# Moving a 192-byte tile ahead of four pools, so that the tiles behind it begin 192 bytes later

## The chip, the cores and the metric

The kernel runs on one core of one Trainium2 chip. The metric is the device time of one execution in microseconds (us). Before the change the median of three runs is 416.2 us (415.88 to 416.37).

## The reference

The kernel computes a gated mix of an attention branch and a dense branch over 2048 tokens of 448 features, all in float32:

```python
g = sigmoid((x * gate_w).sum(-1, keepdims=True))
# branch A: 16 heads of 28; each token attends to the 8 tokens 0, 2, 4 ... 14 places back
qkv = x @ wqkv;  logits = q . k[pos - 2*w] * 28**-0.5;  a = (softmax(logits) . v) @ wo
# branch B
h = relu(x @ w1 + b1) ** 2;  b = h @ w2 + b2          # 448 -> 1792 -> 448
out = g * a + (1 - g) * b
```

## The kernel before, in words

Precision and pairs. Every matrix product is made of three: each operand is split into a high part (`...h`) and a low part (`...l`, or index 1 of a token tile), and high x high, high x low and low x high are added up in PSUM. The contraction of 448 is cut into seven pieces of 64 rows. `side_by_side` (lines 308 to 317) issues two matmuls at a time, one on rows 0 to 63 of TensorE and one on rows 64 to 127, which run beside each other. Below, such a couple is a **pair step**. Line 315 is `nc.tensor.matmul(acc.pt[:, :acc.n], a[rows], w[rows], ...)`: `a` is the stationary operand, which a weight load (LDWEIGHTS) brings into the array, and `w` is the moving operand, which is streamed past it, 448, 450 or 512 columns long.

The stages on TensorE, in order:

- q, k and v (`qkv_first`, `qkv_two`, `run`): four chunks of 512 tokens, of 252 matmuls each (chunk 0: 36 over all 128 rows at line 402, then 180). Stationary: 128 tokens of a chunk's tiles `x{c}_{j}`. Moving: `wqh`, `wql`, `w7h`, `w7l`, 448 columns, or 450 for q, where two columns carry the gate's weights. Chunk 3 has the first steps of the dense branch ahead of its last 24 matmuls.
- The dense branch, in the chunk order 3, 0, 1, 2 (`ORDER`). `h_first` and `h_second`: stationary `w1h`, `w1l`, `w17h`, `w17l`, moving the chunk's token tiles, 512 columns: 4 x 147 = 588 pair steps. `o_part`: stationary the tiles `h{c}_{f}`, moving `w2ah`, `w2al`, `w2bh`, `w2bl`, 448 columns.
- The attention's output times `wo` (`wo_first`, `wo_second`, `wo_end`): stationary the split heads, moving `woh`, `wol`, `wo7h`, `wo7l`, 448 columns.

Beside TensorE, GpSimd (POOL) multiplies q with k (`qk_piece`, line 504) and the weights with v (`av_piece`, line 516) into tiles `pp`, VectorE (DVE) reduces them (lines 508 and 526), ScalarE (ACT) evacuates PSUM and splits operands. Transfers are issued by the SP queue. A planner (`Plan`) with a table of costs writes the order of the instructions out while the program is built; sizes and dependences go into it, addresses don't.

Where tiles lie. Pools are laid out one behind the other in SBUF, in the order of their opening, and a tile's address is the same in all partitions. `const` begins at byte 1152, which is 128 modulo 256, and is 77,312 bytes long, a multiple of 256. Behind it lie `xpool`, `attp`, `smp`, `prodp`, `smallp` (only `zg`, 6 x 8 floats, 192 bytes) and `rawp`. Lines 277 (`pad_a`), 952 (`pad_b`) and 443 (48 floats in `kv_tile`) are fillings of 192 bytes. In the program as built the starts are, modulo 256:

| tiles | role on TensorE | start before | start after |
|---|---|---|---|
| `w1h`, `w1l`, `w17h`, `w17l` | stationary, dense branch | 128 | 128 |
| `w2ah`, `w2al`, `w2bh`, `w2bl`, `woh` ... `wo7l` | moving | 128 | 128 |
| `wqh`, `wql`, `w7h`, `w7l`, all three blocks | moving, q, k, v | 128 | 128 |
| `x0_j`, `x2_j` (pool `phase_a_x`) | stationary, q, k, v | 64 | 64 |
| `x1_j`, `x3_j` (pool `xpool`) | stationary, q, k, v; `x3_j` also moving | **128** | **64** |
| `x0b_j`, `x1b_j`, `x2b_j` in `xpool` | moving, dense branch | **128** | **64** |
| `x0b_3`, `x1b_0`, `x2b_2` (pool `weights_b`) | moving, dense branch | 128 | 128 |
| `h{c}_{f}` (pool `rawp`), `oh`, `ol`, `o7` | stationary | 64 | 64 |
| `o...` in the `pp` tiles, lines 1043 and 1044 | stationary | 64 | 64 |
| q, k, v tiles, `lg`, `pp` | none | **128** | **64** |

Slices of 128 tokens, of 128 columns of `w1`, and the blocks of `wqh` begin at multiples of 256 bytes, so they keep these remainders. The reloaded tokens `x{c}b_j` take the four slots of `xpool` and a fifth one in `weights_b` in turn (`x_reload`, line 945).

Of the kernel before, what the change touches and what calls it, by code (L numbers as in the profile page):

```python
# [7 lines left out]
F32 = mybir.dt.float32  # L8
F32R = mybir.dt.float32r
# [4 lines left out]
S, D, H, DH, W, F = 2048, 448, 16, 28, 8, 1792  # L14
P = 128
NS = 8
# [4 lines left out]
C = HG * DH  # L21
# [16 lines left out]
PP_BUFS = 4  # L38
# [15 lines left out]
class Plan:  # L54
# [29 lines left out]
    def add(self, eng, cost, fn, *deps, prio=MID, at=0.0, port=False, move=None):  # L84
        j = Job()
        j.eng, j.cost, j.fn, j.deps, j.prio, j.port, j.move = eng, cost, fn, [d for d in deps if d], prio, port, move
        j.at, j.done, self.count = max(at, self.now), None, self.count + 1
        j.n = self.count
        self.jobs[eng].append(j)
        return j  # L90
# [88 lines left out]
def gated_mix_kernel(ctx: ExitStack, tc: tile.TileContext, xT, wqkv, w1, w2, wo, b1, b2, out):  # L179
    nc = tc.nc  # L180

    def f32(ap):
        return ap.bitcast(F32)
# [12 lines left out]
    const = ctx.enter_context(tc.tile_pool(name="const", bufs=1))  # L196
# [8 lines left out]
    w2al = const.tile([P, NFA, D], F32R, name="w2al")  # L205
    b2t = const.tile([P, D], F32, name="b2t")
    mask = const.tile([P, NS, W], F32, name="mask")

    xpool = ctx.enter_context(tc.tile_pool(name="xpool", bufs=1))
    attp = ctx.enter_context(tc.tile_pool(name="attp", bufs=1))  # L210
    smp = ctx.enter_context(tc.tile_pool(name="smp", bufs=2))
    prodp = ctx.enter_context(tc.tile_pool(name="prodp", bufs=1))
    smallp = ctx.enter_context(tc.tile_pool(name="smallp", bufs=1))
    zg = smallp.tile([P, 6, NS], F32, name="zg")
    zt, gt, g1t = zg[:, 0:2], zg[:, 2:4], zg[:, 4:6]
    rawp = ctx.enter_context(tc.tile_pool(name="rawp", bufs=2, reuse_waits="tile"))
    biasp = ctx.enter_context(tc.tile_pool(name="biasp", bufs=1))
# [761 lines left out]
    def fin_fetch(par, t):  # L979
        if (par, t) in half:  # L980
            fin_begin(par, t)
# [51 lines left out]
    def wo_split(par, t, hold, loads):  # L1033
        st = Wo()
        st.par, st.t = par, t
        place = "pp" if par and t % 4 else "oh"
        st.place = place
        free = part_last["oh"] if place == "oh" else reduced_all[-PP_BUFS:] + part_last["pp"]
        st.accs = accs = [Acc("m", f"a{par}_{t + r}", D, now=False) for r in range(2)]

        def parts():
            if place == "pp":
                oh, ol, o78 = (prodp.tile([P, C * W], F32R, tag="pp", name=f"o{n}{par}_{t}", bufs=PP_BUFS)[:, 48:48 + n * P]
                               for n in (6, 6, 2))
            else:
                oh, ol, o78 = (bp.tile([P, n * P], F32R, tag=tag, name=f"{tag}{par}_{t}")
                               for tag, n in (("oh", 6), ("ol", 6), ("o7", 2)))
            st.oh, st.ol = (o.rearrange("p (k t n) -> p k t n", k=3, t=2) for o in (oh, ol))
            st.o7, st.o8 = o78[:, :P], o78[:, P:]
            raw = hold[0]  # L1050
            st.full, st.last = raw[:, :6 * P].rearrange("p (k t n) -> p k t n", k=3, t=2), raw[:, 6 * P:]
            nc.scalar.activation(st.oh, st.full, AF.Copy)

        def copied(r):
            accs[r].open()
            st.pv = getattr(st, "pv", []) + [accs[r].pt.rearrange("p (k n) -> p k n", k=4)]
            nc.scalar.activation(st.pv[r][:, 0:3], st.full[:, :, r], AF.Copy)

        a = add(ACT, 847.0, parts, *loads, *free, prio=SOON)
        b = [add(ACT, 486.0, lambda r=r: copied(r), a, *accs[r].after, prio=SOON) for r in range(2)]  # L1060
        b[1].deps.append(b[0])
        c7 = add(ACT, 293.0, lambda: nc.scalar.activation(st.o7, st.last, AF.Copy), b[1], prio=SOON)
        d7 = add(ACT, 262.0, lambda: nc.scalar.activation(st.pv[0][:, 3], st.last, AF.Copy), c7, prio=SOON)
        lows = [add(DVE, 550.0, lambda r=r: nc.vector.tensor_sub(st.ol[:, :, r], st.pv[r][:, 0:3], f32(st.oh[:, :, r])),
                    b[r], prio=SOON) for r in range(2)]
        lows.append(add(DVE, 280.0, lambda: nc.vector.tensor_sub(st.o8, st.pv[0][:, 3], f32(st.o7)), d7, prio=SOON))
        if not par or t == 0:
            raw_last["ot"] = [d7]
        for r in range(2):
            fin_fetch(par, t + r)  # L1070
        st.jobs = [d7, *lows]
        accs[0].after, accs[1].after = (*st.jobs,), (*st.jobs,)
        return st
# [119 lines left out]
    for g in range(2, 2 * NF):  # L1193
        i, f = g // (NF // 2), g % (NF // 2) * 2
# [111 lines left out]
```

## Time and profile before

| | |
|---|---|
| median of three runs | 416.2 us (415.88 to 416.37) |
| the profiled execution's own time | 415.95 us |
| its span, first to last instruction | 414.1 us |
| TensorE matmuls busy | 408.6 us, 3828 matmuls |
| VectorE, ScalarE, GpSimd busy | 258.6, 206.0, 265.8 us |
| mean granted TensorE clock | 0.999 |

The page gives the busy time of each engine, then the span in 40 slices, the chain of work that ended last, and the costliest groups of instructions with the mean duration of one. [...]

### The profile page before, as it was taken

Reading aid. Unit: us, or ns where it says so; the run is one execution under the profiler, and the core shown is the slowest. Engines: PE = TensorE matmul, PEld = TensorE weight load, DVE = VectorE, ACT = ScalarE, POOL = GpSimd, SP = SyncE. Lnnn points to the kernel's source line nnn. Section 1 sums busy time; section 2 is a strip of 40 time slices with the busy share of each in tenths; the row PEclk is TensorE's granted clock in tenths of the full one; section 3 lists DMA queues with packets and bytes.
Section 4 is the critical chain, followed back from the end, with each engine's and each line's share of the span. In section 5 each row is a group of like instructions: output and inputs, shape, how many; then the busy total and the mean of one; then the engine's idle time right before and its main releaser. Section 6 shows DMA issues by size and latency. Waiting matters only on the chain.

```text
span 414.1 us, 9249 instructions
## 1 busy us (share of the span) xinstructions
PE 408.6 (99%) x3828; PEld 404.2 (98%) x3828; DVE 258.6 (62%) x346; ACT 206.0 (50%) x501; POOL 265.8 (64%) x165
## 2 busy tenths in 40 slices
PE   8999999999999999999999999999999999999996
PEld 7999999999999999999999999999999999999995
DVE  4514523484386768777656899786767586593453
ACT  5746766242464665444555435345615344346730
POOL 0000000876969999889999897999998975950000
PEclk9999999999999999999999999999999999999999
DMA  7999999845164433544203669663626022068404
GB/s 242 377 346 295 398 378 372 309 156 205 46 215 188 150 106 132 208 161 152 82 4 127 223 149 310 218 162 64 218 91 232 4 90 85 22 158 157 112 2 178
DMA packets 64555, 73.75 MB, mean 178 GB/s; under 512 B 32321, under 2 KB 57345, under 8 KB 64129
## 3 DMA queue, kind: packets, MB, share of 16 engines
q1 hardware_dynamic: 64224, 72.90, 53.5%
q8 instruction: 30, 0.49, 0.5%
q10 hardware_dynamic: 288, 0.26, 0.2%
q14 instruction: 13, 0.10, 0.1%
HBM read 45.71 MB, written 28.25 MB: 179 GB/s over the span
## 4 chain that ended last, share of the span: by engine, by line
PE 98%; DMA 1%; DVE 0%; ACT 0%; issue 0%
PE b L315 32%; PE h L315 32%; PE qkv L315 23%; PE a L315 7%; PE qkv L402 2%; PE a L1096 1%; DMA wqraw<-wqkv 1%; DVE bt_b L987 0%; ACT wqh L796 0%
## 5 line engine op out<-in xcount | busy, mean ns | idle before, releaser
L504 POOL TENSOR_TENSOR pp<-q,k 128x896 f32<-128x896 f32 x64 | 135.1, 2152 | 86.9 <-DMA k<-k_d 78.4
L516 POOL TENSOR_TENSOR pp<-lg,v 128x896 f32<-128x896 f32 x64 | 118.9, 1962 | 4.3 <-DVE lg L508 2.6
L315 PE MATMUL qkv<-wqh,x 64*128 64x448 f32 (+1 forms) x528 | 91.6, 362 | 0.0
L757 DVE TENSOR_TENSOR h<-h,h 128x512 fp32r<-128x512 f32 x56 | 38.7, 691 | 67.2 <-ACT h L756 66.8
L315 PE MATMUL b<-w2ah,h 64*128 64x448 f32 x448 | 78.8, 359 | 0.0
L315 PE MATMUL b<-w2bh,h 64*128 64x448 f32 x448 | 78.7, 359 | 0.0
L508 DVE TENSOR_REDUCE lg<-pp 128x32 f32<-128x896 f32 x64 | 67.5, 1077 | 14.0 <-POOL pp L504 14.0
L315 PE MATMUL qkv<-wql,x 64*128 64x448 f32 (+1 forms) x264 | 75.2, 362 | 0.0
L315 PEld LDWEIGHTS qkv<-wqh,x 64*128 64x128 f32 x528 | 74.0, 184 | 0.3
L526 DVE TENSOR_REDUCE o<-pp 128x112 f32<-128x896 f32 x64 | 67.2, 1069 | 3.1 <-POOL pp L516 3.1
L315 PEld LDWEIGHTS b<-w2ah,h 64*128 64x128 f32 x448 | 63.8, 184 | 0.0
L315 PEld LDWEIGHTS b<-w2bh,h 64*128 64x128 f32 x448 | 62.9, 184 | 0.2
L315 PE MATMUL b<-w2al,h 64*128 64x448 f32 x224 | 63.1, 358 | 0.0
L315 PE MATMUL b<-w2bl,h 64*128 64x448 f32 x224 | 62.3, 358 | 0.0
L753 ACT ACTIVATE h<-h,b1z 128x512 f32<-128x512 f32 x56 | 36.7, 656 | 41.1 <-PE h L315 41.1
L315 PEld LDWEIGHTS qkv<-wql,x 64*128 64x128 f32 x264 | 44.7, 184 | 0.2
L315 PEld LDWEIGHTS b<-w2al,h 64*128 64x128 f32 x224 | 38.4, 184 | 0.0
L315 PEld LDWEIGHTS b<-w2bl,h 64*128 64x128 f32 x224 | 37.7, 184 | 0.1
L315 PE MATMUL h<-x,w1h 64*128 64x512 f32 x168 | 35.7, 386 | 0.0
L315 PE MATMUL h<-x0b,w1h 64*128 64x512 f32 x168 | 35.6, 386 | 0.0
L337 ACT ACTIVATE st<-qkv 128x448 f32<-128x448 f32 x48 | 24.4, 541 | 21.8 <-PE qkv L315 15.8
L755 ACT ACTIVATE h<-h 128x512 fp32r<-128x512 f32 x56 | 33.5, 598 | 1.5
(132 smaller groups left out, 855.6 us busy)
## 6 DMA issues: line engine op xcount, KB each, us to landing
k<-k_d SPq DMA_DIRECT2D x8, 840.0 KB, 6.1
v<-v_d SPq DMA_DIRECT2D x8, 840.0 KB, 4.7
x_d<-x SPq DMA_DIRECT2D x12, 512.0 KB, 6.4
q_d<-st SPq DMA_DIRECT2D x8, 448.0 KB, 4.8
k_d<-st SPq DMA_DIRECT2D x8, 448.0 KB, 4.7
v_d<-st SPq DMA_DIRECT2D x8, 448.0 KB, 5.5
q<-q_d SPq DMA_DIRECT2D x8, 448.0 KB, 3.3
o_d<-o SPq DMA_DIRECT2D x16, 224.0 KB, 2.2
```

The source lines that it names most:

```text
L315: nc.tensor.matmul(acc.pt[:, :acc.n], a[rows], w[rows], start=acc.todo == acc.all, stop=acc.todo == 1)
L337: nc.scalar.activation(st[0][:, :, t % 2], pt[:, :D].rearrange("p (g c) -> p g c", g=G), AF.Copy)
L402: nc.tensor.matmul(acc.pt[:, :NQ], a, w, start=k == j == 0, stop=False)
L504: nc.gpsimd.tensor_mul(pr.rearrange("p (w c) -> p w c", w=W), q[:, s:s + 1].to_broadcast([P, W, C]), k[:, s:s + W])
L508: nc.vector.tensor_reduce(lgs[i][:, s], pr.rearrange("p (w h d) -> p w h d", w=W, h=HG), axis=AX.X, op=ALU.add)
L516: nc.gpsimd.tensor_mul(pr.rearrange("p (h d w) -> p w h d", h=HG, w=W), lgs[i][:, s][:, :, :, None].to_broadcast([P, W, HG, DH]), vs[i][:, ...
L526: nc.vector.tensor_reduce(o_t[par, s][:, g * C:(g + 1) * C], pr.rearrange("p (c w) -> p c w", w=W), axis=AX.X, op=ALU.add)
L753: a = add(ACT, 656.0, lambda pt=pt, r=r: nc.scalar.activation(pt, pt, AF.Relu, bias=b1t[:, f + r:f + r + 1]), ready, bias_job[0], prio=NEXT)
L755: b = add(ACT, 600.0, lambda pt=pt, hh=hh: nc.scalar.activation(hh, pt, AF.Square), a, prio=NEXT)
L757: low = add(DVE, 690.0, lambda pt=pt, hh=hh, hl=hl: nc.vector.tensor_sub(hl, pt, f32(hh)), a, prio=NEXT)
L1096: nc.tensor.matmul(acc.pt[:, :D], a, w, start=False, stop=acc.todo == 1)
```

## The change

`zg` is allocated at the end of `const` and no longer in a pool of its own behind `prodp`. So `xpool`, `attp`, `smp` and `prodp` begin 192 bytes later, and `rawp` and all behind it stay where they were. The heads that `wo_split` keeps in `pp` tiles lose their offset of 48 floats, so that their addresses stay as they were too. The order of the instructions on each engine, their sizes and their waits are the same before and after: the two programs differ in addresses alone.

```diff
     mask = const.tile([P, NS, W], F32, name="mask")
+    zg = const.tile([P, 6, NS], F32, name="zg")
 
     xpool = ctx.enter_context(tc.tile_pool(name="xpool", bufs=1))
     attp = ctx.enter_context(tc.tile_pool(name="attp", bufs=1))
     smp = ctx.enter_context(tc.tile_pool(name="smp", bufs=2))
     prodp = ctx.enter_context(tc.tile_pool(name="prodp", bufs=1))
-    smallp = ctx.enter_context(tc.tile_pool(name="smallp", bufs=1))
-    zg = smallp.tile([P, 6, NS], F32, name="zg")
     zt, gt, g1t = zg[:, 0:2], zg[:, 2:4], zg[:, 4:6]
...
             if place == "pp":
-                oh, ol, o78 = (prodp.tile([P, C * W], F32R, tag="pp", name=f"o{n}{par}_{t}", bufs=PP_BUFS)[:, 48:48 + n * P]
+                oh, ol, o78 = (prodp.tile([P, C * W], F32R, tag="pp", name=f"o{n}{par}_{t}", bufs=PP_BUFS)[:, :n * P]
                                for n in (6, 6, 2))
```

## The prediction

> **What bounds the kernel now.** The page first: span, busy time, granted clock, and the chain that ended last.
>
> ```profile
> span 414.1 us, 9249 instructions
> ...
> PE 408.6 (99%) x3828; PEld 404.2 (98%) x3828; DVE 258.6 (62%) x346; ACT 206.0 (50%) x501; POOL 265.8 (64%) x165
> ...
> PEclk9999999999999999999999999999999999999999
> ...
> PE 98%; DMA 1%; DVE 0%; ACT 0%; issue 0%
> ```
>
> TensorE has 98% of the chain at an ungated clock. The view of TensorE's waits shows whether something else makes it late:
>
> ```profile
> PE warm L771 <- DVE b1z L768: 1.1, 1, 1.1
> PE qkv L402 <- ACT wqh L796: 0.3, 1, 0.3
> ```
>
> Two waits, 1.4 us, both before the first pair step. From there the end is set by the pace of the pair steps alone, and a change that moves nothing but addresses can act in two ways: by that pace, or by slowing another engine until TensorE must wait for it. The profiled execution took 415.95 us, 1.85 more than its span; the three runs have a median of 416.2.
>
> The chain in order of time gives the pace where nothing disturbs it (dense branch, chunk 1):
>
> ```profile
> 270.33 2.40 PE b L315 x24
> ...
> 274.54 2.72 PE h L315 x24
> 277.26 2.40 PE b L315 x24
> ```
>
> 24 matmuls are 12 pair steps: 200 ns with 448 columns and 226.7 ns with 512. The 64 more columns cost 26.7 ns, 0.417 ns each; 448 x 0.417 is 186.7 and 512 x 0.417 is 213.3, so either form pays the same 13.3 ns beside its columns. Now the four chunks of q, k and v, by windows (stretch, its length, then TensorE's busy time and matmuls, which count those cut by the edges). The first lies inside chunk 0; the second and third run from the first matmul of chunks 1 and 2 to that of the next, found by counting 252; the fourth from the first of chunk 3 to the first of the dense branch, 228 on:
>
> ```profile
> 18.00:30.00 12.00, 12.00 (x123) 12.00 (x122) 2.60 (x5) 6.19 (x18) 0.00 (x0) 1.00 0.95 341
> 31.04:56.78 25.74, 25.74 (x256) 25.63 (x253) 10.33 (x19) 16.66 (x52) 0.00 (x0) 1.00 1.01 355
> 56.78:82.15 25.37, 25.37 (x254) 24.93 (x253) 10.03 (x15) 13.91 (x44) 8.50 (x5) 1.00 0.97 347
> 82.15:105.54 23.39, 23.39 (x231) 23.39 (x228) 15.68 (x10) 8.47 (x29) 17.24 (x10) 1.00 0.50 169
> ```
>
> Chunk 1: 25.74 / 126 = 204.3 ns a pair step. Chunk 2: 25.37 / 126 = 201.4. Chunk 3: 23.39 / 114 = 205.2. For chunk 0, 123 less the three or four that the edges cut are 60 pair steps in 12 us, 200 ns. So the chunks whose tokens start at 128 modulo 256 are slow and the two at 64 are not, though chunks 1 and 2 have the same work and the same DMA load (355 and 347 GB/s), and chunk 3 is slowest with half of it (169). The groups of matmuls within 18 to 30, 34 to 55, 58 to 80 and 84 to 104 us (one stretch inside each chunk, in order) say the same in the mean duration of one:
>
> ```profile
> L315 PE MATMUL qkv<-wqh,x 64*128 64x448 f32 x75 | 11.8, 359 | 0.0
> ...
> L315 PE MATMUL qkv<-wqh,x 64*128 64x448 f32 x80 | 19.7, 363 | 0.0
> ...
> L315 PE MATMUL qkv<-wqh,x 64*128 64x448 f32 x82 | 20.6, 359 | 0.0
> ...
> L315 PE MATMUL qkv<-wqh,x 64*128 64x448 f32 x73 | 18.4, 365 | 0.0
> ```
>
> 359, 363, 359, 365 ns: the same instruction on the same weights, 4 to 6 ns longer where stationary and moving operand both start at 128.
>
> **The change, part by part.** No instruction goes, comes or moves, and no wait or transfer. What remains are four groups of changed addresses.
>
> (a) *Chunks 1 and 3 as stationary operand, 128 to 64.* All weights stay at 128, so the two chunks get the operand starts of chunks 0 and 2. I price that at chunk 2's pace, which runs the same function: chunk 1 wins 126 x (204.3 - 201.4) = 0.37 us, chunk 3 wins 126 x (205.2 - 201.4) = 0.48 us, together 0.85 us. The upper bound is the steady pace of chunk 0, 200 ns: 126 x 4.3 + 126 x 5.2 = 1.2 us. The lower: what chunk 3 takes over chunk 1, 205.2 - 204.3 ns, may be POOL's (busy 17.24 us of 23.39 beside it, not at all beside chunk 1) and stay; then chunk 3 wins 0.37 us too, together 0.7. I take **-0.9 us**, near chunk 2's pace.
>
> [...]
>
> (b) *The same tiles as moving operand of the dense branch, 128 to 64.* Of 588 pair steps 105 read the fifth slot, which stays; 483 change. In the trace every moving operand starts at 128, so this is unseen. What bounds it: at 128 beside stationary `w1` at 128 these steps hold the undisturbed pace, so nothing can be won (226.7 ns is columns plus the 13.3 ns that every form pays). What made 448-column steps longer does not show at 512, with the same equal starts. One reading fits both rows: the weight load of the next step is what is delayed.
>
> ```profile
> L315 PEld LDWEIGHTS qkv<-wqh,x 64*128 64x128 f32 x528 | 74.0, 184 | 0.3
> ...
> L315 PE MATMUL h<-x,w1h 64*128 64x512 f32 x168 | 35.7, 386 | 0.0
> ```
>
> A load takes 184 ns. In a step of 200 it leaves 16 ns, most of which the 13.3 may need; in one of 226.7 it leaves 43. A load late by 4 to 6 ns shows in the first and hides in the second. If that is so, 64 beside 128 hides too. I take 0; the lower end is 0, the upper is the nearest row, chunk 3's 5.2 ns over 200, on 483 steps: +2.5 us. It would show only from a delay of the stream itself.
>
> (c) *q, k, v, `lg` and `pp` tiles, 128 to 64.* POOL's slices of q and k step by 448 bytes, so that the eight pieces of a unit already start at all four remainders 0, 64, 128 and 192. Their durations, minimum, median and maximum, with DVE's below:
>
> ```profile
> L504 POOL TENSOR_TENSOR pp<-q,k x64: 2117/2146/2211, 73.6 to 326.4; 128x896 f32<-128x896 f32 x64
> ...
> L516 POOL TENSOR_TENSOR pp<-lg,v x64: 1904/1958/2034, 118.4 to 365.9; 128x896 f32<-128x896 f32 x64
> ...
> L526 DVE TENSOR_REDUCE o<-pp x64: 1027/1076/1101, 122.2 to 372.3; 128x112 f32<-128x896 f32 x64
> ```
>
> 4% to 7% from shortest to longest over four remainders of the inputs: 0. Only `pp` had one remainder. What hides a loss is the slack of the last heads, by the instructions that write or read the tile `ot` (their durations again, and first and last start) and the time that their loads take to land:
>
> ```profile
> L1023 SPq DMA_DIRECT2D ot<-o_d x16: 591/617/1395, 241.4 to 383.0; - x16
> ...
> L1052 ACT ACTIVATE o<-ot x2: 832/832/832, 389.2 to 396.3; 128x768 fp32r<-128x768 f32 x2
> ...
> DMA to landing us min/median/max: 2.2/3.1/4.9
> ```
>
> The last reduction ends at 373.4, the last load lands at about 383.0 + 3.1, and ACT reads it at 396.3: 10 us to spare behind the load. On 128 pieces that is 78 ns each, a large part of either group's spread; beyond it the end would move one for one.
>
> (d) *`zg`, and the heads in `pp`.* `zg` keeps its remainder, the heads their addresses: 0. Transfers into the moved tiles (token reloads, q, k, v) stay in their places in SP's queue; TensorE waits for none of them now, and the DMA has slack once they begin (a share of 0.50 in chunk 3's window): 0.
>
> The sum is -0.9 us: 415.95 becomes 415.05, and on the runs' median 416.2 becomes **415.3 us**, -0.2%. What is earlier by 0.4 us after chunk 1 and 0.9 after chunk 3 must also be fed earlier; with TensorE waiting for nothing after 5 us I see no feed that tight.
>
> **The rivals.**
>
> *Slower: the moving stream of 512 columns loses at 64.* For it: no row shows a moving operand at 64, and 483 steps are exposed against 252 that win, so a loss of 0.9 us / 483 = 1.9 ns a step turns the sign. Against it: the dense branch was not touched by equal starts, and stationary operands at 64 are read without harm. At 4 to 5 ns a step it gives 1.9 to 2.4 - 0.9, +1.0 to +1.5 us: 417.2 to 417.7 us.
>
> *No change: the start is not the cause.* Chunks 1 and 3 also lie elsewhere (bytes 78,464 to 94,847, against 202,048 to 218,431), and stay there. For it: two places, two paces, so the trace alone cannot part place from remainder. Against it: `h` and the two halves of `w2` lie in other places again and hold 200 ns, all with stationary 64 and moving 128. It gives 416.2 us. [...]
>
> *More is won:* chunks 1 and 3 reach chunk 0's pace, -1.2 us, 415.0 us. This is the end of the forecast's own range.
>
> **How the numbers follow.** A measurement of this kernel can tell about 0.2%, 0.83 us, from no change. Forecast 0.70, with a gain between 0.7 and 1.2 us, two thirds of it beyond 0.83: 0.46 faster, 0.24 same. No change 0.14: 0.13 same, 0.01 slower. Slower dense branch 0.13: all slower. Anything else (a late feed, POOL) 0.03: 0.01 faster, 0.01 same, 0.01 slower. Faster 0.47, same 0.38, slower 0.15. The likeliest case's own range is 415.0 to 415.5. For 8 in 10 the range must take in the case of no change and the scatter of the runs (0.2 to 0.3 us): 414.7 to 416.5; it leaves out the slower rival.
>
> **What would show it.** Right: chunk 1 takes 25.3 to 25.4 us from first matmul to chunk 2's first; the 448-column groups of all four chunks have a mean near 359 ns; h stretches stay at 2.72 us for 24 matmuls and 386 ns; everything after 106 us begins 0.9 us earlier, and TensorE still has no wait after 5 us. Wrong: h groups above 386 ns (first rival), 363 and 365 ns again in chunks 1 and 3 (second), a wait of TensorE for ACT or a DMA (a feed), or POOL pieces beyond 2.25 us.

## The result and the profile after

| | before | after |
|---|---|---|
| median of five runs each | 415.88 us (415.63 to 416.37) | 419.60 us (419.48 to 420.33) |
| span of the profiled execution | 414.1 us | 417.8 us |
| first matmul of chunk 1, 2 and 3; matmul 228 behind chunk 3's first | 31.04, 56.78, 82.15, 105.54 us | 30.93, 56.32, 81.84, 104.96 us |
| start of the last matmul | 409.60 us | 413.33 us |

The change costs 3.7 us: the ratio is 1.0091 [1.008, 1.0103]. The forecast was 415.3 us, a gain of 0.9 us, with a range of 414.7 to 416.5 us; the result lies outside the range and on the other side.

The page after, in the same order as the one before (line numbers are one lower: L314 is the old L315):

```profile
span 417.8 us, 9249 instructions
...
PE 412.6 (99%) x3828; PEld 407.6 (98%) x3828; DVE 254.7 (61%) x346; ACT 206.2 (49%) x501; POOL 271.4 (65%) x165
...
PEclk9999999999999999999999999999999999999999
...
PE 99%; DVE 0%; issue 0%
```

TensorE is again the whole chain, at a mean granted clock of 1.000, but busy 4.0 us longer with the same 3828 matmuls. Its waits after:

```profile
PE warm L770 <- DVE b1z L767: 1.1, 1, 1.1
```

No engine and no transfer holds it up: no new wait came. The time is in the matmuls. Windows of after: the two middle chunks and chunk 3, cut at the same matmuls as in the prediction, then everything from matmul 228 behind chunk 3's first to the start of the last one. (By start time this matmul is the last of q, k and v on one row group; on the other row group the first matmul of the dense branch begins just ahead of it, at 105.41 us before and 104.77 us after.)

```profile
30.93:56.32 25.39, 25.39 (x256) 25.34 (x253) 10.32 (x19) 16.63 (x52) 0.00 (x0) 1.00 1.03 358
56.32:81.84 25.52, 25.52 (x256) 24.77 (x253) 10.47 (x15) 13.91 (x44) 9.29 (x5) 1.00 0.97 346
81.84:104.96 23.12, 23.12 (x231) 22.07 (x229) 9.25 (x8) 8.45 (x29) 15.86 (x7) 1.00 0.54 171
...
104.96:413.33 308.37, 308.37 (x2863) 306.58 (x2861) 211.69 (x281) 148.64 (x330) 245.45 (x142) 1.00 0.44 134
```

The last of these before:

```profile
105.54:409.60 304.06, 304.06 (x2864) 302.24 (x2861) 209.86 (x279) 148.55 (x330) 239.25 (x140) 1.00 0.44 136
```

Chunk 1 went from 25.74 to 25.39 us and chunk 3 from 23.39 to 23.12: the gain is there. Chunk 2, whose operands did not move, lost 0.15. Another 0.11 us was won ahead of chunk 1. Matmul 228 behind chunk 3's first so comes 0.58 us early, and the rest takes 308.37 us in place of 304.06: 4.31 us lost, 0.58 won, 3.73 in all. The chain in order of time shows which stretches lost:

```profile
272.45 2.40 PE b L314 x24
...
276.65 2.79 PE h L314 x24
279.45 2.42 PE b L314 x24
...
283.95 2.41 PE a L314 x24
```

An `h` stretch of 24 matmuls takes 2.79 us, before 2.72. The `b` stretch behind it, with the same operands at the same addresses as before, takes 2.42, before 2.40; the `b` stretch that follows another 448-column stretch (an `a` stretch, the product with `wo`) still takes 2.40. The groups say it per instruction (mean ns of one):

```profile
L314 PE MATMUL h<-x,w1h 64*128 64x512 f32 x168 | 37.0, 392 | 0.0
```

386 ns became 392. The groups of the matmuls of q, k and v inside chunks 1, 2 and 3, in the same stretches as before:

```profile
L314 PE MATMUL qkv<-wqh,x 64*128 64x448 f32 x82 | 20.1, 359 | 0.0
...
L314 PE MATMUL qkv<-wqh,x 64*128 64x448 f32 x82 | 20.4, 361 | 0.0
...
L314 PE MATMUL qkv<-wqh,x 64*128 64x448 f32 x75 | 18.7, 361 | 0.0
```

They were 363, 359 and 365 ns. From the starts of all matmuls, taken on each row group from one start to the next, the dense branch's `h` steps lost 3.6 us: the 483 pair steps with moved tokens went from 226.9 to 233.3 ns, 3.1 us; the 105 of the unmoved fifth slot from 226.7 to 231.1, 0.5 us. The `b` steps lost 0.7 us, from 200.1 to 201.1 ns. From the sixth step of a stretch on, an `h` step with moved tokens went from 226.8 to 233.4 ns, a `b` step from 200.1 to 200.2.

### The profile page after: what moved, and what is told of

Same layout as the page of the kernel before. It is cut to its first block, busy times and chain, and to the rows that moved or that the text cites. A ratio compares the mean times of both kernels' runs of the same rounds, so it can differ in the third digit from the quotient of the medians.

```text
span 417.8 us, 9249 instructions
## 1 busy us (share of the span) xinstructions
PE 412.6 (99%) x3828; PEld 407.6 (98%) x3828; DVE 254.7 (61%) x346; ACT 206.2 (49%) x501; POOL 271.4 (65%) x165
## 4 chain that ended last, share of the span: by engine, by line
PE 99%; DVE 0%; issue 0%
PE h L314 33%; PE b L314 32%; PE qkv L314 23%; PE a L314 7%; PE qkv L401 2%; PE warm L770 1%; PE a L1095 1%; DVE bt_b L986 0%; DVE zero L766 0%; DVE b1z L767 0%
## 5 line engine op out<-in xcount | busy, mean ns | idle before, releaser
L503 POOL TENSOR_TENSOR pp<-q,k 128x896 f32<-128x896 f32 x64 | 137.3, 2184 | 87.3 <-DMA k<-k_d 78.4
L515 POOL TENSOR_TENSOR pp<-lg,v 128x896 f32<-128x896 f32 x64 | 122.7, 2029 | 4.9 <-DVE lg L507 3.0
L314 PE MATMUL qkv<-wqh,x 64*128 64x448 f32 (+1 forms) x528 | 91.0, 361 | 0.0
L314 PE MATMUL b<-w2ah,h 64*128 64x448 f32 x448 | 80.0, 360 | 0.0
L314 PE MATMUL b<-w2bh,h 64*128 64x448 f32 x448 | 79.7, 360 | 0.0
L314 PEld LDWEIGHTS qkv<-wqh,x 64*128 64x128 f32 x528 | 74.2, 184 | 1.0
L314 PE MATMUL qkv<-wql,x 64*128 64x448 f32 (+1 forms) x264 | 74.8, 360 | 0.0
L314 PEld LDWEIGHTS b<-w2ah,h 64*128 64x128 f32 x448 | 65.7, 184 | 0.1
L314 PEld LDWEIGHTS b<-w2bh,h 64*128 64x128 f32 x448 | 64.4, 184 | 0.2
L314 PE MATMUL b<-w2al,h 64*128 64x448 f32 x224 | 64.1, 359 | 0.0
L314 PE MATMUL b<-w2bl,h 64*128 64x448 f32 x224 | 63.1, 359 | 0.0
L314 PEld LDWEIGHTS qkv<-wql,x 64*128 64x128 f32 x264 | 45.5, 184 | 0.5
L314 PEld LDWEIGHTS b<-w2al,h 64*128 64x128 f32 x224 | 39.9, 184 | 0.0
L314 PEld LDWEIGHTS b<-w2bl,h 64*128 64x128 f32 x224 | 38.9, 184 | 0.1
L314 PE MATMUL h<-x,w1h 64*128 64x512 f32 x168 | 37.0, 392 | 0.0
L314 PE MATMUL h<-x0b,w1h 64*128 64x512 f32 x168 | 37.0, 392 | 0.0
L699 ACT ACTIVATE w1h<-w1h 128x2 fp32r<-128x2 f32 x28 | 5.8, 207 | 59.5 <-PE h L314 59.5
```

What stands on the lines that cost most here:

```text
L314: nc.tensor.matmul(acc.pt[:, :acc.n], a[rows], w[rows], start=acc.todo == acc.all, stop=acc.todo == 1)
L503: nc.gpsimd.tensor_mul(pr.rearrange("p (w c) -> p w c", w=W), q[:, s:s + 1].to_broadcast([P, W, C]), k[:, s:s + W])
L515: nc.gpsimd.tensor_mul(pr.rearrange("p (h d w) -> p w h d", h=HG, w=W), lgs[i][:, s][:, :, :, None].to_broadcast([P, W, HG, DH]), vs[i][:, ...
L699: return add(ACT, 205.0, lambda: nc.scalar.activation(ap, f32(ap), AF.Copy), *deps, prio=TURN)
```

## The experiments

Three theories stood before the first runs. **S, the stream**: the moving operand of 512 columns loses at its new start. **R, the rest**: the moved attention tiles slow POOL and DVE and TensorE beside them. **Place**: not the start but the part of SBUF matters. Each edit below is against the kernel before. S had two forms that the change does not part: *start* (the moving operand has to begin at a multiple of 128 bytes) and *distance* (what counts is stationary start minus moving start, modulo 256). By distance the stages of the kernel read: before, `h` steps 0, `b` and chunks 0 and 2 at -64, chunks 1 and 3 at 0; after, `h` steps +64, all of q, k and v at -64. A distance of -64 is the same as +192. Below, a pace is the distance between the starts of one pair step and the next, from the trace. The mean duration of a matmul on the page is another number: 386 ns for the `h` steps before, which start every 226.7 ns.

**e1_rest_only**: all of the change but the tokens.

```diff
     xpool = ctx.enter_context(tc.tile_pool(name="xpool", bufs=1))
+    smallp = ctx.enter_context(tc.tile_pool(name="smallp", bufs=1))
+    zg = smallp.tile([P, 6, NS], F32, name="zg")
     attp = ctx.enter_context(tc.tile_pool(name="attp", bufs=1))
...
-    smallp = ctx.enter_context(tc.tile_pool(name="smallp", bufs=1))
-    zg = smallp.tile([P, 6, NS], F32, name="zg")
...
-                oh, ol, o78 = (prodp.tile([P, C * W], F32R, tag="pp", name=f"o{n}{par}_{t}", bufs=PP_BUFS)[:, 48:48 + n * P]
+                oh, ol, o78 = (prodp.tile([P, C * W], F32R, tag="pp", name=f"o{n}{par}_{t}", bufs=PP_BUFS)[:, :n * P]
```

> zg lies between xpool and attp: the token tiles keep 128 modulo 256, only the q, k, v, lg and pp tiles go to 64. Theory S (the moving stream of 512 columns loses at start 64 beside stationary 128): same as before within 0.3 us, h steps 226.7 ns, chunks 1 and 3 still slow. Theory R (the moved attention tiles get in TensorE's way, or slow POOL until TensorE waits): slower by most of the 3.7 us.

Measured: 415.88 against 415.99 us, ratio 0.9999 [0.999, 1.0008]. R is out: the attention's tiles at 64 cost nothing that these runs could tell (0.4 us either way).

**e2_tokens_only**: the tokens at 64, in another place, and nothing else moved.

```diff
-    xpool = ctx.enter_context(tc.tile_pool(name="xpool", bufs=1))
     attp = ctx.enter_context(tc.tile_pool(name="attp", bufs=1))
...
     zg = smallp.tile([P, 6, NS], F32, name="zg")
+    xpool = ctx.enter_context(tc.tile_pool(name="xpool", bufs=1))
```

> xpool is opened behind zg: the token tiles go to 64, at another place (bytes 113,216 on), the q, k, v, lg and pp tiles keep 128. Theory S: slower by 3.5 to 4 us, like the change, h steps near 233 ns, chunks 1 and 3 gain about 0.6 us. Theory R: no loss, 0.6 us gained. If the place and not the start made chunks 1 and 3 slow, their pace is neither before's nor the change's.

Measured: 419.80 us, ratio 1.0092 [1.0079, 1.0106], with `h` steps at 233.4 ns from the sixth of a stretch on. Chunk 1 takes 25.44 us, so its gain comes too. The tokens carry the whole change, and carry it to another place: place is out, S stands.

**e3_wq_64_later**: the q, k and v weights and, behind them, `x0` and `x2` go 64 bytes on. Chunks 1 and 3 get distance -64 from the other side, chunks 0 and 2 keep it, the dense branch keeps 0.

```diff
+    ap.tile([P, 16], F32, name="pad_w")
     wqh = ap.tile([P, 3, NP + 2 * D], F32R, name="wqh")
```

> A filling of 64 bytes ahead of wqh: the moving operand of q, k, v starts at 192 and the tokens of chunks 0 and 2 at 128, xpool stays at 128. So all four chunks have moving 192 beside stationary 128, 64 apart as 128 and 64 are in the good chunks, the other way round from the change's 64 beside 128. Theory S-distance (what counts is the distance from stationary to moving start, +64 good, -64 bad): all four chunks near 201 ns, 0.7 to 1.2 us faster than before. Theory S-start (a moving operand must start at a multiple of 128): the 504 pair steps lose 5 ns or more, 2.5 us or more slower.

This expectation counts the distance the other way round, moving minus stationary start: its +64 is the -64 of the text.

Measured: 415.23 against 415.99 us, ratio 0.9984 [0.9975, 0.9993]. Chunks 1, 2 and 3 by windows, cut at the same matmuls:

```profile
30.96:56.40 25.44, 25.44 (x256) 25.25 (x253) 10.32 (x19) 16.56 (x52) 0.00 (x0) 1.00 1.02 357
56.40:81.86 25.46, 25.46 (x255) 25.24 (x253) 10.47 (x15) 13.92 (x44) 9.08 (x5) 1.00 0.97 345
81.86:104.99 23.13, 23.13 (x232) 22.86 (x230) 9.23 (x8) 8.45 (x29) 15.75 (x7) 1.00 0.54 171
```

These are the gains of the change, 25.44 and 23.13 us, without a token at 64; the moving weights begin at 192, no multiple of 128, and lose nothing. That speaks for distance and against start. This version is faster than both kernels.

**e4_map**: the dispute by itself. Sixteen pairs of tiles, moving and stationary at 0, 64, 128 and 192 (letters `a` to `d`, `m` and `s`), 48 pair steps each, for 512 columns and for 448.

```python
for n in (512, 448):
    for m in "abcd":
        for s in "abcd":
            for k in range(STEPS):
                for r in range(2):
                    nc.tensor.matmul(y[r][:, :n], stat[s][rows, b * P:b * P + P], mov[m][rows, :n], ...)
```

> Leaves out the whole computation: 48 pair steps for each of four starts of the moving operand (ma, mb, mc, md at 0, 64, 128, 192 modulo 256) beside four of the stationary one (sa to sd, the same), with 512 and with 448 columns, nothing else running. Theory S-distance: the pace depends on the difference of the two letters alone; mc-sb good in both forms, mc-sc good at 512 and some 5 ns longer at 448, mb-sc 6 ns longer at 512. Theory S-start: ma and mc good, mb and md slow whatever the stationary operand. If all 32 have one pace, other engines' traffic is needed for the loss.

Groups of the map, with the moving tile at 0, 64, 128 and 192 and the stationary one at 128 throughout, so distances 128, +64, 0 and -64:

```profile
L43 PE MATMUL ya<-ma,sc 64*128 64x448 f32 x48 | 9.9, 363 | 0.0
...
L43 PE MATMUL ya<-ma,sc 64*128 64x512 f32 x48 | 11.3, 391 | 0.0
...
L43 PE MATMUL ya<-mb,sc 64*128 64x448 f32 x48 | 9.9, 360 | 0.0
...
L43 PE MATMUL ya<-mb,sc 64*128 64x512 f32 x48 | 11.4, 393 | 0.0
...
L43 PE MATMUL ya<-mc,sc 64*128 64x448 f32 x48 | 9.9, 362 | 0.0
...
L43 PE MATMUL ya<-mc,sc 64*128 64x512 f32 x48 | 11.1, 386 | 0.0
...
L43 PE MATMUL ya<-md,sc 64*128 64x448 f32 x48 | 9.8, 359 | 0.0
L43 PE MATMUL ya<-md,sc 64*128 64x512 f32 x48 | 11.2, 388 | 0.0
```

With equal distance the absolute start makes no difference here: the four pairs of each distance agree (mean duration of a matmul of 512 columns: 386 ns at 0 behind the first case, 391 to 393 at +64, 391 at 128, 388 at -64), but for 448 columns at 0, which has two paces (202.7 ns with both starts at 0 or both at 128, 206.7 with both at 64 or 192; e8 has 206.7 at 128, so the start alone does not decide it). The first case began ahead of the full clock (see e12); its steps settle at 226.7 ns behind that.

| distance | 512 columns, ns a pair step | 448 columns |
|---|---|---|
| 0 | 226.7 | 202.7 or 206.7 |
| +64 | 233.4 | 202.2 |
| 128 | 232.4 | 204.0 |
| -64 | 228.9 (233.3 in e10; both in e12) | 200.0 |

So in this map 512 columns are fastest at 0 (226.7 ns) and 448 at -64 (200.0), which is what the kernel before had but for chunks 1 and 3. The change brings those two to their best and takes the 483 steps from their best to their worst: (233.4 - 226.7) x 483 = 3.2 us.

**e5_weights_64, e6_tokens_192, e7_tokens_0**: three more ways to set the starts in the full kernel. The first puts `zg` ahead of all of `const`, so that `w1`, `w2a` and the tokens are at 64 (`h` at distance 0 but for the fifth slot, half of `b` at 0, the other half at -64). The other two split `zg` and open `xpool` between its parts, behind `prodp`: 64 bytes (`zz`) lie ahead of it in e6, 128 bytes (`gg`) in e7. In e5 the heads in `pp` lose their offset, as in the change. The edits of e5 and of e6:

```diff
+    zg = const.tile([P, 6, NS], F32, name="zg")
     w1h = const.tile([P, 3, F], F32R, name="w1h")
...
-    smallp = ctx.enter_context(tc.tile_pool(name="smallp", bufs=1))
-    zg = smallp.tile([P, 6, NS], F32, name="zg")
```

```diff
-    xpool = ctx.enter_context(tc.tile_pool(name="xpool", bufs=1))
...
-    zg = smallp.tile([P, 6, NS], F32, name="zg")
-    zt, gt, g1t = zg[:, 0:2], zg[:, 2:4], zg[:, 4:6]
+    zz = smallp.tile([P, 2, NS], F32, name="zz")
+    xpool = ctx.enter_context(tc.tile_pool(name="xpool", bufs=1))
+    smallq = ctx.enter_context(tc.tile_pool(name="smallq", bufs=1))
+    gg = smallq.tile([P, 4, NS], F32, name="gg")
+    zt, gt, g1t = zz, gg[:, 0:2], gg[:, 2:4]
```

> zg lies at the very beginning of const, so that w1h to w17l, w2ah and w2al go to 64 as well as the tokens. The tokens lie exactly as in the change. Theory S-distance with the map's paces (stationary minus moving start): the 483 steps of the dense branch are at distance 0 again, 226.7 ns, the 105 of the fifth slot at -64, 228.8 ns (+0.2 us); q, k, v keep what the change gained (-0.6 us); the half of the second dense matmul that reads w2ah and w2al goes from -64 to 0, 202.7 to 206.7 ns instead of 200 on 336 steps (+0.9 to +2.2 us). Sum 0.5 to 1.8 us slower than before, some 2 to 3 us faster than the change. Theory S-start (a moving operand at 64 loses): as slow as the change or slower, 3.7 to 6 us.

> xpool behind prodp at 192 modulo 256, everything else as before. Theory S-distance: dense branch at -64, 228.8 ns on 483 steps (+1.0 us), chunks 1 and 3 at +64, 202.3 ns (-0.6 us): 0.2 to 0.8 us slower. Theory S-start: the moving tokens lose 6 ns at 192 as at 64, 3 us or more slower.

> xpool behind prodp at 0 modulo 256. Theory S-distance: dense branch at 128, 232.5 ns on 483 steps (+2.8 us, and up to 1 us more in the steps behind them, as in the change), chunks 1 and 3 at 128, 204 ns (-0.1 us): 2.5 to 3.7 us slower. Theory S-start: 0 is a multiple of 128, so no loss.

| | time, before beside it | ratio | `h` step with moved tokens, from the sixth of a stretch on | the map's pace |
|---|---|---|---|---|
| e5 | 418.78, 415.74 us | 1.0072 [1.0059, 1.0085] | 227.4 ns | 226.7 |
| e6 | 418.32, 415.74 us | 1.0061 [1.0049, 1.0074] | 228.9 ns | 228.9 |
| e7 | 418.65, 415.74 us | 1.0075 [1.0061, 1.0089] | 232.9 ns | 232.4 |

e7 came as expected and ends the start form of S: 0 is a multiple of 128 and loses 2.9 us. e5 and e6 are misses in size, 3.0 and 2.6 us slower. From the sixth step on they keep the map's pace within 1 ns; what they lose more lies in the steps behind a change of the column length. In e5 the `h` steps lost 2.0 us in all where 0.2 was expected, and the first four steps of a stretch take 231 to 234 ns in the mean. In e6 the `b` steps, whose operands did not move, lost 1.2 us, and have 199.8 ns from the sixth step on. So the map's pace is not the whole price.

**e8_fine_map**: the map in steps of 32 bytes, the moving tile at 128 and sixteen stationary tiles 0 to 480 bytes beyond it, for 512, 450 and 448 columns.

> Leaves out the whole computation: the map once more with one moving operand at 128 and sixteen stationary ones 32 bytes further each (sa at 128, sb at 160 ... sp at 96), with 512, 450 and 448 columns. Theory S-distance with a period of 256 bytes: si to sp repeat sa to sh; sa 226.7 ns at 512, sg (-64) 200.0 at 448; the others between 200 and 207, 226.7 and 233.5. A distance of 32 or 96 that is faster than these would be a better place. If the period is longer than 256 bytes, si to sp differ from sa to sh.

Measured: the second half repeats the first, so over these 512 bytes the paces repeat every 256. For 512 columns 0 has 226.7 ns (the first case, which began ahead of the full clock, settles there), -64 has 228.9, all others 232.5 to 234.4. For 450 columns -64 has 200.0 and all others 203.3 to 207.8. For 448, +96 and -64 have 200.0, all others 202.1 to 206.7. No distance is below the paces that the kernel before has in its dense branch.

**e9_tokens_and_w1_64**: the change, and with it `w1` and the fifth slot at 64, so that `h` has distance 0 again while `w2` stays at 128 and the `h` tiles at 64.

```diff
-    w1h = const.tile([P, 3, F], F32R, name="w1h")
-    w1l = const.tile([P, 3, F], F32R, name="w1l")
-    w17h = const.tile([P, F // 2], F32R, name="w17h")
-    w17l = const.tile([P, F // 2], F32R, name="w17l")
...
     mask = const.tile([P, NS, W], F32, name="mask")
+    zg = const.tile([P, 6, NS], F32, name="zg")
+    w1h = const.tile([P, 3, F], F32R, name="w1h")
+    w1l = const.tile([P, 3, F], F32R, name="w1l")
+    w17h = const.tile([P, F // 2], F32R, name="w17h")
+    w17l = const.tile([P, F // 2], F32R, name="w17l")
...
-    smallp = ctx.enter_context(tc.tile_pool(name="smallp", bufs=1))
-    zg = smallp.tile([P, 6, NS], F32, name="zg")
...
-    x_reload(1, 3, 4)
     bw.tile([P, 48], F32, name="pad_b")
+    x_reload(1, 3, 4)
```

The heads in `pp` lose their offset here too, as in the change.

> The change taken to its end: const holds w2ah, w2al, b2t and mask first (at 128), then zg, then w1h to w17l, which so start at 64 as the tokens do; the filling of 192 bytes ahead of the last pool moves ahead of the fifth token slot, which then starts at 64 too. Tokens, q, k, v and pp lie exactly as in the change. Theory S-distance: h steps at distance 0, 226.7 ns, q, k, v at -64, the second dense matmul at -64: 0.6 to 1.0 us faster than before, 4 us faster than the change. If it is the load of the next step that meets the stream, the steps between the two dense matmuls gain too (before: stream of w2 at 128 beside a load of w1 at 128, 448 columns; here beside 64), some 0.2 to 0.4 us more. Theory S-start: the moving tokens at 64 still lose, 3 us or more slower than before.

Measured: 417.04 against 415.92 us, ratio 1.0024 [1.0013, 1.0034]. This undoes only the distance of the `h` steps and gives back 2.6 of the 3.7 us, so the distance of the `h` steps carries most of the loss. The sign was missed: 1.1 us stay lost. `h` settles at 226.7 ns, but only after five longer steps (231, 236, 228, 232 and 231 ns in the mean over its stretches).

**e10_pairing**: couples as in the map, to see what has to share a distance. `c` is 128, `b` is 64; *ahead* is +64, *lone* has one row group, *full* all 128 rows and one matmul a step; two more cases change the starts from one step to the next, two give the row groups different starts.

> Leaves out the whole computation: twelve cases of 48 steps, with 512, then 448 columns (mc, mb: moving at 128, 64; sc, sb: stationary likewise; the first case only warms up). equal mc-sc, ahead mb-sc, behind mc-sb as in the map: 226.7, 233.4, 228.9 ns at 512. inphase: even steps mc-sc, odd steps mb-sb; antiphase: even mc-sb, odd mb-sc. If a stream meets its own step's stationary operand, inphase has 226.7 and antiphase the mean of 228.9 and 233.4, 231; if it meets the load of the next step, which the trace starts 3 ns after it, the other way round. groupsequal: mc-sc in one row group, mb-sb in the other; groupscross: mc-sb and mb-sc; if the row groups meet each other, groupscross is the better one, else 226.7 and 229 to 233. loneequal, loneahead: one row group alone; fullequal, fullahead: 128 rows. If the loss needs two row groups, the lone and full cases do not differ.

```profile
L71 PE MATMUL ya<-mbfullahead,scfullahead 128*128 128x512 f32 x48 | 11.4, 394 | 0.0
...
L71 PE MATMUL ya<-mbloneahead,scloneahead 64*128 64x512 f32 x48 | 11.4, 391 | 0.0
...
L71 PE MATMUL ya<-mcfullequal,scfullequal 128*128 128x512 f32 x48 | 11.2, 392 | 0.0
...
L71 PE MATMUL ya<-mcloneequal,scloneequal 64*128 64x512 f32 x48 | 11.0, 386 | 0.0
```

The case *groupscross* gives the two row groups, in the same stretch, distance -64 (`ya`) and +64 (`yb`):

```profile
L71 PE MATMUL yb<-mbgroupscross,scgroupscross 64*128 64x512 f32 x48 | 11.4, 392 | 0.0
...
L71 PE MATMUL ya<-mcgroupscross,sbgroupscross 64*128 64x512 f32 x48 | 11.1, 388 | 0.0
```

One row group alone, or 128 rows in one matmul, shows the same 226.7 ns at distance 0 and 233.3 at +64. In *groupscross* each row group goes at its own pace, 228.9 and 233.4 ns from start to start, side by side. So the loss needs no second row group beside the first: it goes with the distance between the two operands of one row group. Whether that is the stationary operand of the same step or of the next one stays open: *inphase* took 231.9 ns and *antiphase* 233.3, where either reading of the expectation had 226.7 for one of the two. The case *behind* took 233.3 ns, not the 228.9 of the map.

**e11_all_64_later**: a pad of 64 bytes ahead of `w1h`; every start moves, no distance does.

```diff
+    const.tile([P, 16], F32, name="pad_c")
     w1h = const.tile([P, 3, F], F32R, name="w1h")
```

> A filling of 64 bytes ahead of w1h and nothing else: every tile of before lies 64 bytes later, weights and tokens at 192, h at 128, so that each distance between any two tiles is that of before. If only distances count, within a step and from a step to the load of the next one: the same as before within 0.3 us. If the start itself counts (a multiple of 128 for the moving operand): 3 us or more slower.

Measured: 416.00 against 415.87 us, ratio 1.0002 [0.9993, 1.0011]. Chunks 1 and 2 take 25.74 and 25.37 us, as before. So for the kernel as a whole the starts themselves count for nothing that these runs could tell (0.5 us); the distances do.

**e12_lone_and_lead**: couples in which each matmul opens and closes its own sum, once with one row group at eight distances, once with the second row group started 0 to 384 columns behind the first.

> Leaves out the whole computation. First one row group alone, moving operand at 128, stationary 0, 32, 64 ... 224 bytes further (lonea to loneh), 512, then 448 columns, 48 steps each. Then both row groups at three distances (equal 0, ahead +64, behind -64), where an extra matmul of 0, 64, 128, 256 or 384 columns after the first one gives the second row group a lead of its own (none to most). If the loss lies in the stream and the load of one row group: the lone paces are those of the map (512: 226.7 at 0, 233.4 at +64, 228.9 at -64; 448: 200 at -64), and the lead changes nothing. If the row groups meet each other: the lone case has fewer paces than the map, and the same distance has another pace with another lead, above all behind, which had 228.9 ns in the map and 233.3 ns in the run on pairing.

Measured: in couples of 512 columns, distance 0 has 226.7 and +64 has 233.3 ns whatever the lead: the lead does not set the pace. At -64 the first row group takes 233.3 ns and the second 228.9, at every lead, so both paces of this distance stand side by side in one run.

The lone part came first, and tells nothing on distances: it took 426.7 ns (512 columns) at every one, where e10 has 226.7 and 233.3 for one row group. The couples behind it begin at 427 ns too, and drop to 227 within one case, in which no tile and no instruction changes (starts of the second row group, the first number):

```profile
331.56 0.62 PE L42 MATMUL yb<-mequalnone,sequalnone 64*128 64x512 f32 x1
...
331.99 0.62 PE L42 MATMUL yb<-mequalnone,sequalnone 64*128 64x512 f32 x1
...
332.93 0.39 PE L42 MATMUL yb<-mequalnone,sequalnone 64*128 64x512 f32 x1
...
333.16 0.39 PE L42 MATMUL yb<-mequalnone,sequalnone 64*128 64x512 f32 x1
```

The first record of the granted clock in this trace, full speed, stands at 332.5 us. In e4 and e10 the first record stands at 14.1 and 9.1 us, and there too the steps drop from 427 to 227 ns. So the lone part of e12, with the same 427 ns, is taken to have run ahead of the full clock; the trace holds no record of the clock for that time, though the views print 1.00 there.

**e13_switch**: the longer steps at the edges, with no other engine at work. Rounds of 12 pair steps of 448 columns (moving 128, stationary 64) and 12 of 512 columns, in eight cases.

```python
for mv, st in tiles.values():
    for part in range(2 * ROUNDS):
        n = 512 if part % 2 else 448
        m, t = (mv, st) if part % 2 else (mw, sh)
        for k in range(STEPS):
            for r in range(2):
                nc.tensor.matmul(y[part % 2][r][:, :n], t[rows, b * P:b * P + P], m[rows, :n], ...)
```

> Only couples of matmuls run, and nothing of the reference's computation: eight cases of six rounds each, a stretch of 12 pair steps of 448 columns (moving at 128, stationary at 64) and then one of 12 of 512 columns, whose moving and stationary tiles start at (128, 128), again (128, 128), (64, 128), (64, 64), (0, 0), (192, 192), (192, 128) and (0, 128). The question is whether the longer steps beside a switch come from the addresses. If what counts at a switch is the distance between the stream that runs and the load that comes in, the three cases of equal starts other than 128 have the same 226.7 ns inside their 512-column stretches as (128, 128) but a round (24 matmuls of each form, about 5120 ns) that is 20 to 60 ns longer, the excess lying in the first steps behind a switch. If the longer steps come from other engines of the full kernel, the four cases of equal starts have the same round within 5 ns. In both, (64, 128) has a round some 80 ns longer, (0, 128) some 70 and (192, 128) some 26 or, at its second pace, 80.

Windows of rounds 2 to 5 of the first seven cases, four rounds of 48 matmuls each, in the order of the expectation:

```profile
18.22:38.70 20.48, 20.48 (x194) 19.19 (x192) 0.00 (x0) 0.00 (x0) 1.00 0.00 1
48.94:69.42 20.48, 20.48 (x194) 19.19 (x192) 0.00 (x0) 0.00 (x0) 1.00 0.00 1
79.84:100.70 20.86, 20.86 (x194) 19.24 (x192) 0.00 (x0) 0.00 (x0) 1.00 0.01 2
110.99:131.60 20.61, 20.61 (x194) 19.22 (x192) 0.00 (x0) 0.00 (x0) 1.00 0.01 2
141.96:162.66 20.70, 20.70 (x195) 19.23 (x193) 0.00 (x0) 0.00 (x0) 1.00 0.00 1
173.00:193.72 20.72, 20.72 (x195) 19.26 (x193) 0.00 (x0) 0.00 (x0) 1.00 0.00 1
204.06:224.75 20.69, 20.69 (x194) 19.23 (x192) 0.00 (x0) 0.00 (x0) 1.00 0.01 2
```

A round of the kernel before's starts (128, 128) takes 20.48 / 4 = 5.120 us, 12 x 200 + 12 x 226.7 ns: its switches are free. The three cases with the same distances inside the stretches but another start across the switch, (64, 64), (0, 0) and (192, 192), take 5.153, 5.173 and 5.180 us from the starts of the matmuls. The steps of (64, 64) run 231, 236, 228, 233, 231 and then 226 to 227 ns: e9's pattern within 1 ns, with no other engine beside it. In the other two cases it takes longer until they settle, eight to ten steps. They run through one sequence, entered at different points: (0, 0) takes 228, 235, 233, 236, 224, 231, 236, 228, 233 and 231 ns ahead of 226 to 227, and (64, 64) its last five. So the addresses on both sides of a switch make the longer steps, and not a feed of the full kernel. A change of addresses is not the only way to them, though: the first case of e8, whose tiles stay the same, takes 235, 233, 236, 224, 231, 236, 228, 233 and 231 ns when the full clock has come, and then 226 to 227. The changed kernel's starts, (64, 128), take 5.217 us: 97 ns a round more, of which 81 lie in the 512-column stretch and 15 in the 448-column one, whose operands are the same in all cases. The last two cases lose by their distance: (192, 128), the last line above, takes 5.173 us, 53 ns more and between the two values expected, and (0, 128) 5.190 us, the 70 ns more that were expected. As an estimate, the 483 changed `h` steps of the dense branch are 40 such stretches; at 97 ns they give 3.9 of the 4.3 us that it lost.

## Why the prediction was wrong

*What bounds the kernel: right.* TensorE's pace alone, no new wait, a mean granted clock of 1.000.

*(a), chunks 1 and 3: right in cause and sign, a little too large.* They won 0.35 and 0.27 us, 0.62 together, under the lower bound of 0.7; the forecast was 0.85, taken as 0.9. Chunk 1 came to 201.5 ns a step, as priced. Chunk 3 came to 202.8 where 201.4 was priced, and on the 114 steps of its window, not 126. What it took over chunk 1 stayed (1.3 ns, before 0.9), as the lower bound had it; whether by POOL, no run shows. Chunk 2 lost 0.15 us, which the sum had as nothing: its group of matmuls rose from 359 to 361 ns a matmul though its operands stayed, and e3 has 25.46 us for it as well. Why, stays open. e3 and e10 bear the cause out, since they change nothing but start addresses and move the pace: chunk 1 from 25.74 to 25.44 us in e3, 512-column steps from 226.7 to 233.3 ns in e10.

*(b), the moving tokens of the dense branch: the step that failed.* The prediction put it so: "One reading fits both rows: the weight load of the next step is what is delayed", and so "64 beside 128 hides too. I take 0". Both rows were read right, that 448-column steps lose at equal starts and 512-column ones do not. The reading was wrong. No load late by some ns hides behind a longer stream here: the step itself grows from 226.8 to 233.4 ns, the loads stay at 184 to 185 ns, and which distance is bad depends on the number of columns. 0 is the best for 512 (226.7 ns) and a bad one for 448 (202.7 or 206.7, against 200.0 at -64). From one row of 512 columns, at distance 0, nothing could be said about +64; it had been named unseen and then priced at one end of its range. The term taken as 0 measured 4.3 us. The upper end, 5.2 ns on 483 steps, was too low too: 6.6 ns inside the stretches, and on top the unchanged steps next to each switch, which no bound took in (0.5 us in `h` steps of the fifth slot and 0.7 us in the `b` steps, together 1.2 of the 4.3).

*(c) and (d), the attention's tiles, `zg` and the heads: right in what they do to the time.* e1 measures them alone at nothing. The pieces after, against 2146 and 1958 ns before (minimum, median, maximum):

```profile
L503 POOL TENSOR_TENSOR pp<-q,k x64: 2113/2143/3934, 72.6 to 329.0; 128x896 f32<-128x896 f32 x64
```

```profile
L515 POOL TENSOR_TENSOR pp<-lg,v x64: 1926/2015/2167, 118.0 to 369.5; 128x896 f32<-128x896 f32 x64
```

The second group is 57 ns longer in the median, 3.6 us over its 64 pieces, but TensorE waits for none of it. One piece of the first group took 3.93 us, beyond the 2.25 that the prediction named as a sign of being wrong; single long pieces stand in other runs too (3.09 us in e11, which took as long as before).

*The slower rival* came true in its place, the 512-column stream, and in the sign that shows it: `h` groups above 386 ns. Its price of 4 to 5 ns a step was 6.6, so that its 417.2 to 417.7 us fell short of the 419.6, and its condition, a moving start at 64, was not the rule: in e9 the moving tokens are at 64 and settle at 226.7 ns. *The no-change rival*, place, fell with e2.

What stays open: why a distance is good for 448 columns and bad for 512; why 512 columns at -64 have 228.9 or 233.3 ns; which step's stationary operand the distance counts from; why a disturbed stretch runs through five to ten such steps before it settles.

## What to carry to other kernels

Where TensorE is the bound with a weight load for every matmul, take the start of the stationary tile minus the start of the moving tile modulo 256 as a parameter of its own, for each matmul length (226.7 to 234.4 ns a step at 512 columns in e4 and e8), and measure it with 48 couples of the same length before moving a tile; then keep the relation between neighbouring stages too. When a change moves tiles to mend one stage, list every role in which the same tiles appear: here 240 steps won 0.6 us, 483 others lost 3.1, and the unchanged steps beside them 1.2. An operand relation that no row of the profile shows deserves the width of the effect on its neighbours, in both directions, and not the end that a single explanation gives.

## What the runs showed of the hardware that was not expected

- The pace of fp32 matmuls of 64 rows went with the start distance of their operands modulo 256 bytes, 226.7 to 234.4 ns at 512 columns and 200.0 to 206.7 at 448, at a mean granted clock of 0.989 and 0.993 and with nothing of the reference's computation beside them (e4, e8). With equal distance the absolute start made no difference in e4, but for 448 columns at distance 0, and none in e11 (ratio 1.0002).
- A change of starts between neighbouring stretches cost 33 to 60 ns in a round of one 448-column and one 512-column stretch, even where both have their best distance (e13). The longer steps behind it, 224 to 236 ns, follow one sequence, which e8's first case shows too, where the clock and no address changed.
- One row group alone took as long per step, 226.7 ns, as two beside each other, and two with different distances each went at their own pace, 228.9 and 233.4 ns (e10).
- Matmuls on one row group alone, from the start of the program on, stayed at 426.7 and 373.3 ns a step (512 and 448 columns) for over 320 us, ahead of the first record of the full clock; it came 3.7 us after the second row group joined (e12). What brought it, no run shows.
